# Chunk-selecting attention with a gMLP block: two instead of four head pairs as row halves, half of the stores from GpSimd, and another written-out order

## The chip, the cores and the metric

The kernel runs on one core of a Trainium2 chip. The metric is the device time of one execution in microseconds. A core has five engines that run their own instruction streams and meet only through semaphores: TensorE (PE; matmuls and transposes into PSUM), VectorE (DVE), ScalarE (ACT; exponentials, GELU, evacuation of PSUM), GpSimd (POOL) and SyncE (SP, which here only issues DMAs). The five runs of the kernel before took 216.78 to 218.61 us, median 218.06 us.

## The reference

The input is q, k, v of shape (4, 8, 768, 64): four batches, eight heads, 768 positions. Attention sees only six chunks of 32 keys for each query. They are chosen by an upper bound of the scores:

```python
k_min = np.min(k_chunks, axis=3); k_max = np.max(k_chunks, axis=3)
ub = np.sum(np.maximum(q[:, :, :, None, :] * k_min[:, :, None, :, :],
                       q[:, :, :, None, :] * k_max[:, :, None, :, :]), axis=-1)
ub = np.where(causal, ub, -1e9)
top_chunks = np.argsort(ub, axis=-1)[..., -top_k:]
scores = np.where(sel & (pos[:, None] >= pos[None, :]), scale * q @ k^T, -1e9)
attention = softmax(scores) @ v
```

The heads are then put side by side, x of shape (4, 768, 512), and go through a gMLP block:

```python
h = gelu(x @ w_in)                      # 512 -> 1024, then halves u and v
v_n = (v - mean(v)) / sqrt(var(v) + 1e-6) * g_ln
v_s = einsum('ts,bsd->btd', w_sg, v_n) + b_sg   # 768 x 768 over the positions
out = x + (u * v_s) @ w_out
```

## The kernel before

The 32 heads are taken in 16 pairs; four pairs make one batch, and one gMLP block (b = 0 to 3) follows each four pairs. Every step of the work is one named operation (`P.op`, line 142), a short run of instructions on one engine. A table `ORDER` (from line 18) holds all names in one sequence. `arrange` (L183) walks it, appends each operation to its engine's stream, gives it the PSUM tile number that stands behind the colon, and puts it on another engine where the name carries `@dve`, `@act` or `@pool`. `link` (L214) works out the semaphore waits. So the order on each engine is fixed by the table, and an engine that waits holds back all that stands behind it on that engine. The numbers `cost=` and `prio=` were read by the search that wrote the table; on the chip they do nothing. `FILL` puts a few dummy matmuls (L1041) ahead of some operations, once their PSUM tile is free.

The names, with p a pair, h a head, b a block:

- `lk`, `lq`, `lv` (L499): loads of k, q, v, each head by itself, 192 KB, issued by SP. At most six of them are in flight (`WINDOW`): each waits for the sixth before it to land.
- `kt`, `qt` (L509 to L545): transposes of half a pair's k or q by TensorE. `kn`, `kx` (L530) are the chunk minima and maxima on DVE, `kw` (L541) their difference. `qe`, `qr` (L519, L555 to L564) write q transposed, and its positive part.
- `ub` (L614) makes the upper bounds of one or two pairs in PSUM. `ut`, `uc`, `um`, `ud`, `uq` (L623 to L648, all DVE) transpose them, cut the future, find the sixth largest, and write a row mask `Dt`. Pairs 0 and 1 are selected alone, all others two by two.
- Scores, two ways. `pair_half` (L677, pairs below `NHALF`): k and q of both heads stay as one tile of 128 rows (`KP`, `QP`, written by `ke` and `qc`), and the two heads' products are matmuls over 64 rows each, placed in the upper and lower half of the array (L726). The mask is added by extra matmuls over 32 rows (L719) that read `Dt` directly. One tile `s2.0` holds both heads. `head_full` (L743, all other pairs): head by head, the mask rows sit with k and q in one operand of 96 or 128 rows (`KA`, `QA` or `KB`, `QB`), so one matmul does both (L766). For that `ka`/`kb` evacuate k in two pieces, `qa`/`qb` (L570, L572) copy q, and the rows of `Dt` are copied into `QA` and `QB` by four small DMAs a pair, `d2.00` to `d15.11` (L658, SP), 18 KB each.
- `e` (L736, L770): the exponential on ACT. There are two PSUM tiles of scores, so the second tile after this one waits for it. `af` (L672, POOL): the causal triangle on the diagonal blocks. `vc` (L577, POOL): v to bf16.
- `pv`, `pd` (L787, L795): values, off and on the diagonal. `xr`, `xs` (L804, L813): division by the sum. `xt` (L819): the transpose of x, by SP's transposing DMA, or by TensorE with the copy `xe` for batch 0 and the last one.
- gMLP: `hv` (L853) the v half for 128 positions, four matmuls of 512 columns; `gv` GELU; `bs`, `ba`, `re`, `rp`, `rm`, `rn`, `vh` (L863 to L891) the normalization; `hu`, `gu` (L900, L906) the u half; `pt` (L920) the product with w_sg, six matmuls of 384 columns; `vs`, `gm` (L927, L933) scale, bias and gate; `ou` (L943) the product with w_out, four matmuls; `oa` (L950, DVE) adds x into one of three buffers `osb`; `os` (L955) stores it, 256 KB, from SP. These operations share four PSUM tiles with the transposes, `ub` and `pv`.
- Weights: `win`, `wsg`, `wo` (L962 to L990) are loaded by GpSimd. `wt`, `we` (L980, L985): w_sg transposed by TensorE, six blocks, copied by DVE.

A gMLP operation may stand anywhere in the table among those of the next pairs' attention. In the table before, the first `hv` stands after the selection of pairs 4 to 7 (`ub4`, `ub6`) and after the tiles of heads 8 and 10.

## Time and profile before

| | |
|---|---|
| five runs, median | 218.06 us (216.78 to 218.61) |
| the profiled execution | 216.78 us |
| its span, first to last instruction | 215.0 us |
| PE, DVE, ACT, POOL busy | 202.9, 174.2, 170.5, 118.3 us |
| TensorE's granted clock, mean | 0.995 |
| HBM read and written | 24.77 and 6.29 MB |

The page gives for each engine the time in which it had an instruction running. Matmuls overlap their predecessors' ends, so the record of one is longer than the step from one to the next: a pt matmul is recorded with 326 ns, while 48 of them in a row took 7.80 us, 163 ns each. Costs of TensorE's work are therefore taken from the chain of work that ended last, which lists pieces by the steps between them (start, length, engine, line, how many instructions). In that chain, "SPq" is an issue by SP, and a piece "DMA" is the time from an issue to its landing. A row of a DMA's issue gives the median time to landing.

### The profile page before, as it was taken

How to read it: one execution, taken by the hardware profiler on the slowest of the kernel's cores; microseconds unless marked ns; L12 is line 12 of the kernel's file. 1: busy time of each engine (PE TensorE's matmuls, PEld its weight loads, DVE VectorE, ACT ScalarE, POOL GpSimd, SP SyncE). 2: the span in 40 equal slices, each digit the busy share in tenths (PEclk: the TensorE clock that was granted, in tenths of full speed). 3: DMA queues.
4: the chain of work that ended last, by engine and by line, in shares of the span. 5: the costliest groups of instructions: out<-in, count | busy, mean ns of one | idle time of the engine just before them, and what ended most of it. 6: DMA issues, size and time to landing. Idle time of an engine off the chain costs nothing.

```text
span 215.0 us, 6168 instructions
## 1 busy us (share of the span) xinstructions
PE 202.9 (94%) x2362; PEld 132.1 (61%) x2362; DVE 174.2 (81%) x544; ACT 170.5 (79%) x287; POOL 118.3 (55%) x177
## 2 busy tenths in 40 slices
PE   6688998999999999999999999999999999999990
PEld 2456765567667776865566778764657787445640
DVE  1999999998897978899979999889896558584871
ACT  2469899999989999988998788999997888377000
POOL 3242858968776897915415898303737667030530
PEclk9999999999999999999999999999999999999997
DMA  7999999999889979999469852910172303403034
GB/s 148 220 218 199 213 234 218 147 171 176 155 195 193 216 129 182 268 129 228 94 172 241 204 138 51 232 40 2 38 181 70 109 34 77 146 0 146 5 146 148
DMA packets 92542, 31.78 MB, mean 148 GB/s; under 512 B 85984, under 2 KB 88800, under 8 KB 92512
## 3 DMA queue, kind: packets, MB, share of 16 engines
q1 hardware_dynamic: 90496, 28.62, 61.4%
q0 software_dynamic: 2016, 2.75, 8.7%
q8 instruction: 19, 0.31, 0.6%
q14 instruction: 11, 0.09, 0.1%
HBM read 24.77 MB, written 6.29 MB: 144 GB/s over the span
## 4 chain that ended last, share of the span: by engine, by line
PE 69%; ACT 14%; DVE 7%; DMA 5%; SPq 2%; issue 1%; DVEq 0%
PE PSG L920 14%; PE PSC L766 11%; PE PSG L512 8%; PE PSG L853 7%; PE PSG L943 6%; PE PSG L787 6%; PE PSG L900 5%; PE PSG L614 3%; DMA out_dram<-osb 3%; ACT uT L906 3%; PE PSC L726 3%; PE PSC L719 2%; PE PSG L795 2%; DMA qn<-in_q_dram 2%; ACT E L770 2%; ACT L1046 2%
## 5 line engine op out<-in xcount | busy, mean ns | idle before, releaser
L770 ACT ACTIVATE E<-PSC 128x1024 bf16<-128x1024 f32 (+1 forms) x72 | 62.4, 917 | 7.7 <-PE PSC L766 7.3
L672 POOL TENSOR_SCALAR_AFFINE_SELECT E<-E 128x768 bf16<-128x768 bf16 (+3 forms) x40 | 29.5, 749 | 19.2 <-ACT E L770 10.8
L530 DVE TENSOR_REDUCE W<-PSG 128x12 f32<-128x384 f32 x64 | 34.0, 545 | 4.6 <-PE PSG L512 4.1
L920 PE MATMUL PSG<-wsgT,vhat 128*128 128x384 bf16 x192 | 35.2, 326 | 0.2 <-DVE vhat L891 0.2
L933 POOL TENSOR_TENSOR uT<-vsT,uT 128x384 bf16<-128x384 f32 x24 | 22.6, 950 | 12.7 <-DVE vsT L927 12.4
L927 DVE SCALAR_TENSOR_TENSOR vsT<-PSG,glnT,bsgbc 128x384 f32<-128x384 f32 x32 | 19.6, 611 | 10.5 <-PE PSG L920 10.4
L920 PEld LDWEIGHTS PSG<-wsgT,vhat 128*128 128x128 bf16 x192 | 18.0, 98 | 10.8 <-DVE vhat L891 0.4
L943 PE MATMUL PSG<-woutb,uT 128*128 128x512 bf16 x96 | 23.8, 379 | 0.0
L736 ACT ACTIVATE E<-PSC 128x1024 bf16<-128x1024 f32 (+3 forms) x26 | 21.7, 864 | 2.6 <-PE PSC L726 2.3
L900 PE MATMUL PSG<-xT,winb 128*128 128x384 bf16 x128 | 22.6, 326 | 0.0
L853 PE MATMUL PSG<-winb,xT 128*128 128x512 bf16 x96 | 22.0, 379 | 0.4 <-DVE osb L950 0.4
L577 POOL CAST vx<-vn 128x768 bf16<-128x768 f32 x16 | 13.6, 849 | 14.8 <-DMA vn<-in_v_dram 14.8
L950 DVE TENSOR_TENSOR osb<-PSG,XS 128x512 f32<-128x512 f32 x24 | 16.5, 688 | 5.5 <-PE PSG L943 3.8
L787 PE MATMUL PSG<-vx,E 128*128 128x65 bf16 x480 | 19.7, 193 | 0.6 <-ACT qT L519 0.6
L787 PEld LDWEIGHTS PSG<-vx,E 128*128 128x128 bf16 x480 | 17.7, 97 | 2.9 <-ACT qT L519 0.8
L766 PE MATMUL PSC<-QB,KB 128*128 128x128 bf16 (+2 forms) x168 | 19.1, 246 | 0.3 <-ACT E L770 0.3
L766 PE MATMUL PSC<-QA,KA 96*128 96x128 bf16 (+2 forms) x168 | 19.0, 245 | 0.3 <-ACT E L770 0.3
L858 ACT ACTIVATE vgb<-PSG 128x512 f32<-128x512 f32 x24 | 13.9, 594 | 5.4 <-PE PSG L853 5.3
L873 POOL TENSOR_TENSOR rstd<-rstd,neghalf 128x3 f32<-128x3 f32 x8 | 7.1, 891 | 20.0 <-DVE rstd L869 10.2
L900 PEld LDWEIGHTS PSG<-xT,winb 128*128 128x128 bf16 x128 | 12.4, 98 | 9.2 <-ACT uT L906 0.4
L863 DVE BATCH_NORM_STATS2 stats<-vgb 128x6 f32<-128x512 f32 x24 | 15.8, 678 | 1.8 <-ACT vgb L858 1.6
L512 PE MATMUL PSG<-identF,kn 128*128 128x128 f32 x96 | 15.5, 279 | 1.1 <-DMA kn<-in_k_dram 0.5
(85 smaller groups left out, 389.8 us busy)
## 6 DMA issues: line engine op xcount, KB each, us to landing
kn<-in_k_dram SPq DMA_DIRECT2D x32, 192.0 KB, 4.4
qn<-in_q_dram SPq DMA_DIRECT2D x32, 192.0 KB, 4.4
vn<-in_v_dram SPq DMA_DIRECT2D x32, 192.0 KB, 4.1
out_dram<-osb SPq DMA_DIRECT2D x24, 256.0 KB, 2.7
winb<-in_moe_w_in_dram POOLq DMA_DIRECT2D x4, 256.0 KB, 6.4
vhat<-in_moe_w_sg_dram POOLq DMA_DIRECT2D x3, 192.0 KB, 4.3
xT<-in_moe_w_sg_dram POOLq DMA_DIRECT2D x3, 192.0 KB, 5.9
woutb<-in_moe_w_out_dram POOLq DMA_DIRECT2D x4, 128.0 KB, 4.3
```

The lines of the kernel that those rows point to most:

```text
L512: r = e.matmul(t.ap()[:, 128 * j:128 * j + 128], src[:, 3 * hf + j].rearrange("p i d -> p (i d)"), identF[:], is_transpose=True)
L530: P.op(f"k{'nx'[m]}{p}.{hf}", "dve", lambda d, t=t, m=m, op=op, cs=cs: d.tensor_reduce(W[w][:, m, cs.start // 32:cs.stop // 32], t.ap()[:, ...
L672: P.op(f"af{h}.{r}", "pool", lambda g, ev=ev, cnt=cnt: g.affine_select(ev, ev, pattern=[[0, cnt], [1, 128]], compare_op=ALU.is_ge, fill=0. ...
L736: P.op(f"e{p}.{c}", "act", lambda e, t=t, o0=o0, nn=nn: e.activation(E[:, slot:slot + 2, o0:o0 + nn], t.ap().rearrange("p (i x) -> p i x", ...
L766: r = e.matmul(t.ap()[:, o:o + n], kt_[rows, 128 * kb:128 * kb + 128], qt_[rows, q0:q0 + n], start=True, stop=True, skip_group_check=True)
L770: P.op(f"e{h}h.{c}", "act", lambda e, t=t, c0=c0, c1=c1: e.activation(E[:, es, c0:c1], t.ap()[:, 0:c1 - c0], ACTF.Exp, scale=SCALE), write ...
L787: r = e.matmul(t.ap()[:, 65 * qb:65 * qb + 65], E[:, es, a:a + 128], vx[w][:, kb, i, :], start=first, stop=False, skip_group_check=True)
L853: r = e.matmul(t.ap()[:, 0:F], xT[s][:, dk, 128 * qt:128 * qt + 128], winb[:, dk, F:DFF], start=(dk == 0), stop=(dk == NDK - 1))
L900: r = e.matmul(t.ap()[:, 0:TG], winb[:, dk, 128 * fb:128 * fb + 128], xT[s][:, dk, TG * tg:TG * tg + TG], start=(dk == 0), stop=(dk == NDK ...
L920: r = e.matmul(t.ap()[:, 0:TG], vhat[s][:, sb, 128 * fb:128 * fb + 128], wsgT[:, sb, TG * tg:TG * tg + TG], start=(sb == 0), stop=(sb == N ...
L933: return d.tensor_tensor(gT[s][:, fb, TG * tg:TG * tg + TG], vsT[vs][:], uT[s][:, fb, TG * tg:TG * tg + TG], op=ALU.mult)
L943: r = e.matmul(t.ap()[:, 0:DM], gT[s][:, fb, 128 * qt:128 * qt + 128], woutb[:, fb, :], start=(fb == 0), stop=(fb == NF - 1))
```

## The change

- `NHALF` goes from 4 to 2: pairs 2 and 3 use `head_full`; they get `ka`/`kb`, `qa`/`qb` and the `d` copies. They are selected with 288 query columns instead of 320.
- `WPE` goes from all six to blocks 0, 1, 2: `wt3`, `wt4`, `wt5` become transposing DMAs on SP.
- One load `lv` for both heads of a pair. The buffer `vn` is laid out by head, and `vc` reads it rearranged.
- `hv`, `pt` and `ou` become two operations each (`hv`+`hw`: three and one matmul; `pt`+`pu`: three and three; `ou`+`ov`: two and two) in the same PSUM tile; each piece waits only for its own inputs. Their matmuls are as many as before.
- A store may be issued by GpSimd (`os...@pool`). Eleven are: os0.1, os0.5, os1.3, os1.4, os1.5, os2.1 to os2.4, os3.0, os3.1.
- Two `rT` buffers instead of three, smaller selection buffers, and a dummy matmul that reads 128 columns four times over instead of 512 columns.
- `KDMA = 16` and the buffers `KS` belong to a path for pairs from 16 on, of which there are none.
- The whole table `ORDER`, and `FILL`, are others. The first `hv` now stands ahead of the preparation of pairs 6 and 7 (in part), of `ub6`, and of the tiles of heads 8 and 10. The last gMLP block's `ou` pieces stand between its `pt` pieces.

```diff
-FILL = {"kt1.1": 7, "kt0.1": 4, "qt0.1": 1, "qt2.1": 3, "ou3.4": 1, }
+FILL = {"kt1.1": 7, "kt0.0": 4, "qt0.1": 4, "qt2.0": 3, "s0.2": 1, "ub2": 1, }
...
+                if o.dma is not None:
+                    self.dma_sems[o.dma].remove(o.idx)
+                    o.dma += "_" + eng
+                    self.dma_sems.setdefault(o.dma, []).append(o.idx)
...
-    NHALF = 4
+    NHALF = 2
...
-    WPE = range(NT)
+    WPE = (0, 1, 2)
...
+            if nm == "vn":
+                P.op(f"lv{p}", "sp", lambda e: e.dma_start(
+                    dst[s][:], bass.AP(src.tensor, 2 * p * S * DH, [[DH, 128], [128 * DH, 2 * NT], [1, DH]])),
+                    writes=[(nm, s, 0), (nm, s, 1)], dma=f"{nm}{s}", bulk=True, cost=(640, 1780), prio=prio)
+                return
...
-                def hv(e, t=t, qt=qt):
-                    for dk in range(NDK):
...
+                for nm, dks in (("hv", range(NDK - 1)), ("hw", (NDK - 1,))):
+                    def hv(e, t=t, qt=qt, dks=dks):
+                        for dk in dks:
...
+                    P.op(f"{nm}{b}.{qt}", "pe", hv, reads=[("xT", s, dk, qt // 3) for dk in dks] +
+                         [("winb", dk) for dk in dks], alloc=[t] if nm == "hv" else [], ps=[] if nm == "hv" else [t],
+                         cost=c_pe([F] * len(dks)), prio=prio + qt)
...
+                    for nm, sbs in (("pt", range(3)), ("pu", range(3, NT))):
...
+                    for nm, fbs in (("ou", range(2)), ("ov", range(2, NF))):
...
+                    P.op(f"os{b}.{qt}", "sp", store, reads=[("osb", os_)], dma=f"o{os_}", cost=(640, 500), prio=pq,
+                         alt={"pool": dict(fn=store, cost=(600, 500))})
```

The end of the new table, from the last block's first `pt` on, and of the old one from its last two `pt` on:

```diff
-pt3.11:3 vs3.10 gm3.03 pt3.13:0 gm3.10@dve pt3.12:2 vs3.11 vs3.13 gm3.11 ou3.1:1 vs3.12 ou3.0:3 oa3.1 gm3.12 ou3.2:0
-os3.1 oa3.0 gm3.13 os3.0 oa3.2 ou3.4:2 os3.2 ou3.3:1 oa3.4 ou3.5:3 os3.4 oa3.3 os3.3 oa3.5 os3.5
+rp3.1 pt3.01:2 gu3.20 hu3.10:1 gu3.01 rn3.1 os2.4@pool vh3.4@dve pt3.00:0 gu3.10 pt3.10:3 vh3.3@dve vh3.5 pt3.02:1
+pu3.00 pu3.01 vs3.00 pu3.02 vs3.01 gm3.00 pu3.10 vs3.02 pt3.03:0 gm3.01 pu3.03 pt3.11:2 vs3.03 gm3.02 pu3.11 vs3.10
+ou3.2:1 gm3.03@dve ou3.0:0 pt3.13:3 vs3.11 gm3.10 ov3.0 pu3.13 oa3.0 gm3.11 ou3.1:2 vs3.13 ov3.2 ov3.1 oa3.2 gm3.13
+pt3.12:0 oa3.1 pu3.12 os3.2 os3.0@pool ou3.4:3 vs3.12 ou3.3:1 os3.1@pool ou3.5:2 gm3.12@dve ov3.5 ov3.3 oa3.5 ov3.4
+oa3.3 os3.5 oa3.4 os3.3 os3.4
```

The stretch of the new table between the selection of pairs 2 and 3 and the first tile of head 4:

```
uc2.10 uq2.0 qt4.0:1 af0.1 e0.6 um2.1 kt4.0:0 d2.01 af2.2 s1.0:1 qe4.0 af1.1 kb3.0 kn4.0 d2.00 win2 qt4.1:1 e1.0 ud2.1
d3.00 kt4.1:2 vx10 af1.0 s1.3:0 uq2.1 kx4.0 kb3.1 qb2 d2.11 s1.2:1 e1.3 ka4.0@dve lq5.1 pv1:3 af3.0 kn4.1 d2.10 pd1
e1.2 af0.2 kb4.0@dve s1.6:0 d3.11 iA0 kx4.1 e1.6 pv0:0 d3.01 xr1 s1.4:1 xs1 ka4.1 af3.1 lq5.0 pd0 vc1 e1.4 s4h.1:0 xr0
```

## The prediction

> **What bounds the kernel now.** I read the page first, then the busy time cut at the places where the gMLP blocks begin, then the chain that ended last, and the rows of single shapes last.
>
> ```profile
> span 215.0 us, 6168 instructions
> PE 202.9 (94%) x2362; PEld 132.1 (61%) x2362; DVE 174.2 (81%) x544; ACT 170.5 (79%) x287; POOL 118.3 (55%) x177
> PE 69%; ACT 14%; DVE 7%; DMA 5%; SPq 2%; issue 1%; DVEq 0%
> ```
>
> TensorE has 12.1 us of its span without work, and the chain runs over it for 69%. Where these 12.1 us lie shows in stretches of time (columns: PE, its weight loads, DVE, ACT and POOL busy, granted clock, DMA share, GB/s):
>
> ```profile
> 0.00:15.50 15.50, 11.41 (x112) 6.17 (x112) 10.27 (x45) 7.16 (x15) 5.67 (x16) 1.00 1.15 194
> 15.50:55.08 39.58, 38.03 (x684) 26.09 (x684) 36.83 (x135) 37.34 (x62) 26.77 (x47) 1.00 1.05 194
> 55.08:98.60 43.52, 43.52 (x478) 30.06 (x477) 36.69 (x97) 40.78 (x77) 32.53 (x44) 1.00 0.99 186
> 98.60:184.50 85.90, 85.00 (x961) 57.07 (x960) 72.06 (x232) 75.54 (x117) 46.20 (x62) 1.00 0.50 120
> 184.50:209.90 25.40, 24.98 (x134) 12.76 (x133) 17.62 (x37) 9.64 (x18) 7.11 (x9) 1.00 0.21 76
> 209.90:215.00 5.10, 0.00 (x0) 0.00 (x0) 0.69 (x1) 0.00 (x0) 0.00 (x0) 0.78 0.40 147
> ...
> 62.30:84.00 21.70, 21.70 (x228) 15.79 (x227) 17.48 (x54) 21.43 (x41) 17.67 (x24) 1.00 0.90 182
> ```
>
> Idle TensorE: 4.1 us at the start, 1.6 us up to the first gMLP, 0, 0.9, 0.4, and 5.1 us after the last matmul. So TensorE's work is the time, except in the head and the tail. But the reader should see the last row too: ACT is busy for 21.43 of 21.70 us inside the first gMLP. What leaves TensorE there counts only if ACT has less to do as well.
>
> **The change, part by part.** The sum is made against the profiled execution: 216.8 us, span 215.0 us, 1.8 us around it. The median of the five runs is 218.06 us, 1.3 us above it; I carry the difference over to the median.
>
> *Pairs 2 and 3 as full heads.* Twelve half tiles leave TensorE. In the chain each is a mask piece (L719) and a product piece (L726); three of them:
>
> ```profile
> 38.74 0.32 PE PSC L719 x4
> 39.06 0.33 PE PSC L726 x4
> ...
> 41.24 0.32 PE PSC L726 x4
> ...
> 42.04 0.33 PE PSC L719 x6
> 42.37 0.33 PE PSC L726 x6
> ...
> 50.71 0.60 PE PSC L766 x7
> ...
> 51.50 0.44 PE PSC L766 x4
> ...
> 53.85 0.45 PE PSC L766 x7
> 54.29 0.67 PE PSG L980 x12
> 54.97 0.28 PE PSC L766 x3
> ```
>
> The twelve L719 pieces between 34.5 and 47.7 us add up to 3.36 us, the twelve L726 pieces to 3.63 us: 6.99 us for two pairs. A full head is three tiles of 0.45, 0.44 and 0.28 us, 1.17 us; four heads cost 4.68 us. TensorE gains 2.3 us, and the chain of before passes through all of it.
>
> A rule that speaks against this: the Trainium skill, "TensorEngine Tiling (Array Packing)", Theoretical Speedup, says that a contraction of at most 64 rows, packed in tiles, runs up to twice as fast. By it the 21,504 packed columns of these pairs would take 4.5 us at 2.4 columns per ns, and dropping them would bring nothing. The trace disagrees: 1,024 packed columns took 0.32 us (L726 at 41.24), as many unpacked ones 0.44 us, 1.4 times the pace and not twice. The measurement decides.
>
> *Transposes of w_sg.* Three of six go from TensorE to the transposing DMA: 12 matmuls are 0.67 us above, so six are 0.335 us, three blocks 1.0 us. Their copies (L985, 544 ns) leave DVE. SP issues three transposes more at 1.25 us each (the row of xT<-XS); pt0.10, the first that reads them, stands more than twelve operations of TensorE later in the new order, so a landing of 2.8 us is covered. If it were not, pt would wait up to 2.8 us.
>
> *Selection of pairs 2 and 3* with 288 columns instead of 320: 1.24 to 1.13 us on TensorE, 0.1 us. *The dummy matmul ahead of ou3.4* goes: 216 ns, 0.2 us. Five other dummies are added ahead of 15 us and around ub2, in waits for loads and tile slots; if those waits are gone, they cost 5 x 0.216 = 1.1 us; I take 0.
>
> *hv, pt and ou in two pieces.* No matmul is added; only what a piece waits for is less. In before, ACT and hu tiles filled these waits, so I take 0, but for one place:
>
> ```profile
> 181.17 0.47 SPq L823
> 181.69 4.10 DMA out_dram<-osb
> 185.82 0.70 DVE osb L950
> 186.57 4.49 PE PSG L853 x20
> ```
>
> A store behind a transposing DMA held a buffer, the addition behind it held a PSUM tile, and TensorE waited some 0.5 us before hv3.0. The new order issues that store (os2.1) from GpSimd, and puts ou pieces in front of hv3. I take -0.4 (0 to -0.5).
>
> *Eight Dt copies more.* Full heads read the selection rows from QA and QB, so pairs 2 and 3 now wait for uq, an SP issue and a landing. In the first 60 us such copies landed in 3.8 to 6.1 us, median 4.8, behind the loads, and an issue takes 0.6 us. Head 4 needs two: 2 x 0.6 + 4.8 = 6.0 us. TensorE's work between uq2.0 and s4h.1 in the new order is qt4 and kt4 (4 x 0.33), five tiles of pair 1 (2.6 us) and pv1, pd1, pv0, pd0 (1.3 us): 5.2 us of cover. So I take +0.8; below, 0 (a landing of 2.3 us, the median of QB<-Dt); above, 6.1 + 1.2 - 5.2 = 2.1 us for each of four heads, 8.4 us. Queued on SP behind a late copy are the loads of q for pair 5 and of v for pairs 2 and 3; qt5.1 stands more than ten operations later.
>
> *Where the first gMLP lies.* It begins before pairs 6 and 7 are prepared. Six exponentials (four of 1.02, two of 0.70 us: 5.5 us) and about 1 us of evacuations come into the stretch that has ACT at 94%; TensorE gets 4.4 us more there (two heads 2.3, selection 1.1, seven transposes 2.3, less four such operations that leave, 1.3). ACT goes to 47.3 us beside 47.9 us of TensorE. That can be no wait at all; above, if ACT keeps the 2.7 us of idle time that it has there now, 47.3 + 2.7 - 47.9 = 2.1 us, and 3.0 us with the evacuations that wait for DVE. I take +0.8, below the middle, as 40.78 of 43.52 us made TensorE wait for nothing. The stretch ahead of it has, by the same rows, 7.4 us less ACT and 7.9 us less DVE against 7.5 us less TensorE: no gain, no loss.
>
> *Eleven stores by GpSimd.* An issue is 0.55 us (row of the w_out DMAs), 6.1 us in all; with two qa/qb copies for each qc and three gm more, POOL gets some 10.6 us, beside 97 us of idle time. What is late is the buffer. At the end os3.0 and os3.1 queue on POOL behind gm3.13 (0.91 us) and oa3.3, oa3.4 need their buffers. Counted from pt3.12's start, os3.1 is issued by 1.0 us; oa3.4 could start at 4.1 us. A landing of 2.0 us (SP's stores at the end) is hidden, 4.3 us (the w_out loads on POOL's queue) costs 1.2, 6.4 us (w_in) 3.3 us. The three additions (0.61 us apart) also end 0.3 us further behind TensorE than now. I take +0.5 (0.3 to 3.6), nearest to SP's store, since size and direction are the same.
>
> The Trainium skill, "DMA: Bandwidth & Descriptors", SWDGE vs HWDGE vs iDMA, would leave plain copies to SP, as GpSimd builds descriptors in software; its fit (Anatomy of one DMA) of 2.0 us plus bytes over 436 GB/s gives an estimate of 2.6 us for 256 KB, by which the term would be +0.3. No row here shows a store by GpSimd.
>
> *Merged v loads, casts reading v by head, no early ones on half pairs:* SP issues 16 fewer; POOL waited 14.8 us for v without anyone on the chain waiting for POOL. 0 (-0.3 to +0.5).
>
> Sum: -2.3 - 1.0 - 0.1 - 0.2 - 0.4 + 0.8 + 0.8 + 0.5 = -1.9 us: span 213.1, profiled run 214.9, median 216.1 us.
>
> **Rivals.**
> - *ACT takes over* from 15 to 95 us. ACT's work there falls by 0.8 us only, TensorE's by 3.1. For it: 21.43 of 21.70 us busy. Against: over 15.5 to 98.6 us ACT still idles 5 us. The 2.3 us between them are lost in place of the 0.8 above: 217.6 us, no change; with the 3.0 us of its upper end 218.3.
> - *Slower: the Dt rows of pairs 2 and 3 come late*, between 28 and 40 us. For it: 4.8 us landing with the DMA queues at 1.05 share. Against: by 24 us the first 24 loads are through (192 KB at 217 GB/s, 0.9 us each), and a wait for head 4 gives cover to head 5. With 1.4 us for each of four heads, 5.6 in place of 0.8: 220.9 us. From 1.0 us a head (3.9 us in all) it is slower by over 0.5%.
> - *GpSimd's stores land like w_in*, 6.4 us: 3.6 in place of 0.5: 219.2 us; at 4.3 us 217.1.
> - *Everything is covered*: no wait for Dt, none for ACT: 214.4 us.
>
> **How the numbers follow.** Forecast 0.47 (own range 214.9 to 217.4), ACT 0.19, Dt rows 0.14, stores 0.07, all covered 0.13. About 0.5%, 1.1 us, is what a measurement of this kernel can tell; its five runs lie 1.8 us apart. Below 217.0: of the forecast 0.39, all covered 0.13, of ACT and stores 0.04: 0.56. Above 219.1: Dt rows 0.13, the slow ends of ACT and of the stores 0.10: 0.23. Between: 0.21. The range goes from a little under the covered case (0.07 left out) to the middle of the slow cases (0.12 left out): 213.4 to 219.9 us.
>
> **What would show it.** After: TensorE's idle time around 12 us with 3.4 us less work; no L719 after 30 us; L766 ahead of 30 us without an idle time put down to QA<-Dt; the first L853 near 47 us; ACT's busy share from there above 95%, TensorE's idle time there below 1.5 us; the GpSimd stores' landing near 3 us, and the last additions without a wait for out_dram. It is wrong if TensorE idles over 3 us between 15 and 47 us (Dt rows), over 2 us in the first gMLP (ACT), or if DVE waits for out_dram by more than 2 us in all.

## The result and the profile after

The changed kernel took 218.7 us (median of 38 executions, 214.9 to 221.8), the kernel before 217.39 us (median of 75, on the same chips). The ratio is 0.998 with a 95% interval of 0.9956 to 1.0001: no change that this measurement can tell, where 216.1 us and a gain of 0.9% were forecast. (Medians here and below are over all executions; ratios and their intervals leave out those over 1.5% above the fastest of their kernel, here 27 of the changed kernel's 38, and by the medians it is 0.6% slower.) The profiled execution of the changed kernel took 220.9 us; it is longer than the median by 2.2 us, and a second profile of the same kernel below (219.3 us, span 217.5) shows the same picture in the same places.

What TensorE waited or lost is counted in the text from the steps between the starts of its matmuls. That gives some 0.2 us more for each wait than the tables of waits do, because the record of a matmul outlasts its step.

The page of the changed kernel: its span, the engines' busy time, the rows of 40 slices for TensorE, its granted clock and the DMA engines, and the chain's shares.

```profile
span 219.2 us, 6002 instructions
...
PE 204.4 (93%) x2288; PEld 137.5 (63%) x2288; DVE 171.0 (78%) x539; ACT 170.3 (78%) x283; POOL 128.4 (59%) x193
...
PE   6898689999998999997999999999999999999990
...
PEclk9999955799999999999999999999999999999999
DMA  7999966999187899996789439997101152421033
...
PE 78%; DMA 7%; DVE 7%; SPq 2%; ACT 2%; issue 1%; DVEq 0%
```

TensorE has less to do and is busy for longer, 204.4 us against 202.9. The clock row says why: slices 6 to 8 are not at 9. Stretches of time of the same kernel (columns as in the prediction: length, PE, its weight loads, DVE, ACT, POOL busy, granted clock, DMA share, GB/s), cut where the clock changes and where the gMLP blocks begin:

```profile
15.50:27.35 11.85, 9.02 (x157) 5.63 (x157) 11.20 (x56) 10.72 (x18) 9.70 (x19) 1.00 1.11 204
27.35:41.00 13.65, 12.79 (x143) 9.64 (x144) 7.64 (x22) 7.84 (x12) 6.34 (x13) 0.50 0.76 154
41.00:53.20 12.20, 12.02 (x235) 10.12 (x233) 10.04 (x25) 11.89 (x21) 11.33 (x17) 1.00 1.14 219
53.20:103.90 50.70, 48.48 (x544) 33.82 (x541) 43.45 (x130) 47.03 (x82) 32.63 (x46) 1.00 0.87 164
103.90:150.70 46.80, 46.48 (x534) 32.33 (x526) 41.68 (x128) 43.56 (x73) 25.34 (x35) 1.00 0.84 177
150.70:190.00 39.30, 39.30 (x453) 26.20 (x446) 29.26 (x103) 33.72 (x48) 26.34 (x36) 1.00 0.31 84
190.00:213.80 23.80, 23.76 (x133) 12.34 (x129) 16.68 (x38) 8.25 (x16) 10.03 (x14) 1.00 0.18 67
213.80:219.20 5.40, 0.00 (x0) 0.00 (x0) 1.03 (x2) 0.00 (x0) 0.00 (x0) 0.93 0.39 147
```

For 13.65 us, ahead of the first gMLP block, TensorE ran at half of its clock; before, it had the full clock from the start to the last matmul. The first `hv` stands at 53.2 us, where about 47 was expected, and the first gMLP stretch takes 50.7 us, where the prediction's working gives 48.7 (47.9 of TensorE and 0.8 of waits). From 104 us on the kernel goes as forecast or a little better. What TensorE waited for most between 15.5 and 53 us, from the table of its waits (engine, line, what ended the wait; us in all, times, longest):

```profile
PE PSG L531 <- DMA kn<-in_k_dram: 1.8, 1, 1.8
PE PSC L747 <- DVE Dt L676: 1.3, 2, 1.0
```

And the chain in front of the longer one (start, length, what):

```profile
17.80 0.55 SPq L516
18.34 0.04 issue
18.39 1.54 SPq L522
19.93 0.04 issue
19.97 1.04 SPq L516
21.01 0.04 issue
21.05 7.02 DMA kn<-in_k_dram
28.07 0.14 issue
28.21 0.87 PE PSG L531 x3
```

L531 is a transpose, here `kt4.0`; its k (`lk4.1`) was issued at 21.05 us, behind both merged v loads (L516) and a q load, and landed 7.0 us later. The other wait is `s1.1`'s, for the row mask of pair 1 (L676), which DVE makes in a stretch where it is busy for 11.20 of 11.85 us.

Some steps of the prediction can be read directly. The half tiles (L747 and L754 here) end with pair 1. No wait of TensorE here is for `QA<-Dt`. The issue rows of the stores:

```profile
out_dram<-osb SPq DMA_DIRECT2D x13, 256.0 KB, 2.3
out_dram<-osb POOLq DMA_DIRECT2D x11, 256.0 KB, 2.8
```

GpSimd's stores land in 2.8 us, SP's in 2.3, and the tail after the last matmul is 5.4 us against 5.1.

### The profile page after: what moved, and what is told of

It is laid out like the page before. It is cut to its first block, busy times and chain, and to the rows that moved or that the text cites. A ratio compares the mean times of both kernels' runs of the same rounds, so it can differ in the third digit from the quotient of the medians.

```text
span 219.2 us, 6002 instructions
## 1 busy us (share of the span) xinstructions
PE 204.4 (93%) x2288; PEld 137.5 (63%) x2288; DVE 171.0 (78%) x539; ACT 170.3 (78%) x283; POOL 128.4 (59%) x193
## 4 chain that ended last, share of the span: by engine, by line
PE 78%; DMA 7%; DVE 7%; SPq 2%; ACT 2%; issue 1%; DVEq 0%
PE PSG L950 14%; PE PSC L794 14%; PE PSG L881 9%; PE PSG L929 9%; PE PSG L531 8%; PE PSG L975 7%; PE PSG L815 6%; DMA kn<-in_k_dram 5%; PE PSG L642 3%; DMA out_dram<-osb 3%; PE PSG L823 2%; DVE osb L982 2%; SPq L522 1%; PE PSC L754 1%; DVE W L549 1%
## 5 line engine op out<-in xcount | busy, mean ns | idle before, releaser
L798 ACT ACTIVATE E<-PSC 128x1024 bf16<-128x1024 f32 (+1 forms) x84 | 73.7, 919 | 6.5 <-PE PSC L794 5.8
L950 PE MATMUL PSG<-wsgT,vhat 128*128 128x384 bf16 x192 | 38.0, 326 | 0.4 <-DVE KB L540 0.3
L964 POOL TENSOR_TENSOR uT<-vsT,uT 128x384 bf16<-128x384 f32 x27 | 25.0, 934 | 9.1 <-DVE vsT L958 9.0
L975 PE MATMUL PSG<-woutb,uT 128*128 128x512 bf16 x96 | 25.8, 379 | 0.0
L794 PE MATMUL PSC<-QA,KA 96*128 96x128 bf16 (+2 forms) x196 | 24.1, 254 | 0.0
L794 PE MATMUL PSC<-QB,KB 128*128 128x128 bf16 (+2 forms) x196 | 22.7, 246 | 0.0
L531 PE MATMUL PSG<-identF,kn 128*128 128x128 f32 x96 | 17.3, 299 | 2.3 <-DMA kn<-in_k_dram 2.3
L794 PEld LDWEIGHTS PSC<-QA,KA 96*128 96x128 bf16 x196 | 15.3, 101 | 5.6 <-issue 0.6
L794 PEld LDWEIGHTS PSC<-QB,KB 128*128 128x128 bf16 x196 | 14.6, 98 | 5.4 <-issue 0.5
L599 POOL CAST QB<-qT 64x768 bf16<-64x768 f32 x14 | 11.7, 838 | 10.0 <-ACT qT L538 9.4
```

What stands on the lines that cost most here:

```text
L531: r = e.matmul(t.ap()[:, 128 * j:128 * j + 128], src[:, 3 * hf + j].rearrange("p i d -> p (i d)"), identF[:], is_transpose=True)
L794: r = e.matmul(t.ap()[:, o:o + n], kt_[rows, 128 * kb:128 * kb + 128], qt_[rows, q0:q0 + n], start=True, stop=True, skip_group_check=True)
L798: P.op(f"e{h}h.{c}", "act", lambda e, t=t, c0=c0, c1=c1: e.activation(E[:, es, c0:c1], t.ap()[:, 0:c1 - c0], ACTF.Exp, scale=SCALE), write ...
L950: r = e.matmul(t.ap()[:, 0:TG], vhat[s][:, sb, 128 * fb:128 * fb + 128], wsgT[:, sb, TG * tg:TG * tg + TG], start=(sb == 0), stop=(sb == N ...
L964: return d.tensor_tensor(gT[s][:, fb, TG * tg:TG * tg + TG], vsT[vs][:], uT[s][:, fb, TG * tg:TG * tg + TG], op=ALU.mult)
L975: r = e.matmul(t.ap()[:, 0:DM], gT[s][:, fb, 128 * qt:128 * qt + 128], woutb[:, fb, :], start=(fb == 0), stop=(fb == NF - 1), skip_group_c ...
```

## The experiments

Two theories went first. *Clock*: the two early waits cost little themselves, but they make the chip halve TensorE's clock. *ACT*: the gain is lost in the first gMLP, which ACT fills. All ratios are to the kernel before, run beside it on the same chip.

**The changed kernel again (e0_after).** No edit; 12 executions.

> The changed kernel once more, on the chip of the runs beside it. Theory gate: TensorE's granted clock is 0.5 for some 10 to 14 us between 24 and 41 us in most executions, its time stays within 0.5% of before (ratio 0.995 to 1.005). Theory ACT (the first gMLP block, where ACT is full, takes the gain): the same ratio, and executions without a half clock are no shorter than those with one.

Measured: 218.42 us (216.14 to 221.9), ratio 1.0009 [0.9974, 1.0044]. Profile: span 217.5 us, clock 0.5 from 26.1 us for 13.65 us again. Over its 12 executions the mean clock lay between 0.961 and 0.992; 35 executions of the kernel before had 0.991 to 1.0. Most executions lose their clock, not only the profiled ones.

**Dummy matmuls in the two waits (e1_fill).**

```diff
-FILL = {"kt1.1": 7, "kt0.0": 4, "qt0.1": 4, "qt2.0": 3, "s0.2": 1, "ub2": 1, }
+FILL = {"kt1.1": 7, "kt0.0": 4, "qt0.1": 4, "qt2.0": 3, "s0.2": 1, "ub2": 1, "s1.1": 4, "kt4.0": 9, }
```

> Dummy matmuls are put into the two waits of TensorE ahead of the half clock: 4 ahead of s1.1, 9 ahead of kt4.0. Nothing else changes, and TensorE still waits as long for the k load of pair 4. Theory gate: no half clock between 10 us and the end, the first hv starts near 48 us instead of 53, the span is some 4 us shorter than the changed kernel's (ratio to before 0.975 to 0.985). Theory ACT: under 1 us shorter, ratio 0.993 to 1.0, since ACT sets the pace from 16 us on.

Measured: 217.3 us (215.58 to 219.68), ratio 0.9973 [0.9938, 1.0008], span 214.4 us. The clock row of its page:

```profile
PEclk9999999999999999999999999999999999999999
```

More work on TensorE, and 1.1 us less in the median than e0_after, 3.1 us less in the profile. (The intervals of the two ratios overlap, so the 1.1 us are rough.) The first gMLP stretch is 49.5 us here as in e0_after, so what was gained lies ahead of it. (The 50.7 us of the first profile hold a wait of 1.4 us near the stretch's end, at `pv14`, for an addition that waited for a store's buffer; one later profile, e12_q6_only, has it again.) But the median is only level with the kernel before: the clock is one part.

**An earlier k for pair 4 (e2_loads).** On SP: lk4.0 **lk4.1** lq4.1 **lq4.0** lv0 lk5.0 lv1 lk5.1.

```diff
-... lk4.0 ... lk5.0 ... lq4.1 ... lv0 ... lq4.0 ... lv1 ... lk4.1 ... lk5.1
+... lk4.0 ... lk4.1 ... lq4.1 ... lq4.0 ... lv0 ... lk5.0 ... lv1 ... lk5.1
```

> Five loads change places: the second k load of pair 4 and the first q load go ahead of the two double v loads. Theory gate: the 2.0 us wait ahead of kt4.0 goes, and with it the half clock: 4 to 6 us shorter than the changed kernel, ratio to before 0.970 to 0.985. If the clock halves all the same (the 1.0 us wait ahead of s1.1 stays), only the 2 us wait is won. Theory ACT: under 1 us shorter.

Measured: 217.99 us (214.93 to 220.17), ratio 0.9975 [0.9934, 1.0016]. `kt4.0` no longer waits, yet the clock is halved from 26.4 us for 10.24 us. TensorE's waits of 0.5 us and more between 15.5 and 50 us:

```profile
PE PSC L747 <- DVE Dt L676: 1.0, 1, 1.0
PE PSG L531 <- ACT KA L538: 0.7, 1, 0.7
PE PSG L642 <- POOL W L568: 0.6, 1, 0.6
```

And the clock row of the page:

```profile
PEclk9999956999999999999999999999999999999998
```

Waits of 1.0 us and less, the longest of them 2 us ahead of the fall, were enough here.

**All stores from SP (e3_sp_stores).** The eleven `@pool` behind `os` names taken away.

> All 24 stores go from SP again, at the same places in the order. If the stores by GpSimd took the gain (additions waiting for a buffer), this is 1 to 3 us shorter than the changed kernel. Theories gate and ACT: within 0.7 us of it, and the half clock is there as before.

Measured: 217.92 us (215.77 to 221.68), ratio 0.9996 [0.9961, 1.0031]; span 214.6 us with 6.83 us of half clock from 27.9 us; tail 5.2 us. Who issues the stores makes no difference that shows.

**Three w_sg transposes on SP, alone, in the kernel before (e4_before_wt).**

```diff
-    WPE = range(NT)
+    WPE = (0, 1, 2)
```

(with `we3`, `we4`, `we5` taken out of the table).

> The kernel before, with one part of the change alone: three of its six w_sg transposes (wt3, wt4, wt5) go from TensorE to SP's transposing DMA. My prediction's term: TensorE's path loses 12 matmuls, 1.0 us, so the median falls from 217.3 by 0.6 to 1.1 us (ratio 0.995 to 0.997), and the span of an undisturbed profile from 215.0 to about 214.0. Rival (SP's queue has no room): the three issues of 1.25 us hold loads behind them on SP between 45 and 85 us, TensorE waits for pair 8 and later, and nothing is gained (ratio 0.999 or more), with a wait for a load (in_k_dram, in_q_dram or wsg) ending a TensorE idle time of over 0.5 us between 60 and 100 us.

Measured: 222.12 us (217.67 to 224.33). The ratio, 1.0071 [1.0015, 1.0127], rests on two of twelve executions; by the medians it is 1.023. The rival's direction, and more than its size: the part takes 1.0 us from TensorE's work, and it cost 4.9 us. But the mechanism is not the rival's: TensorE did not wait for a load that an issue held up, but for a transposing DMA itself. The landings of the three transposing DMAs, from the view of the tile `wsgT`:

```profile
DMA to landing us min/median/max: 3.2/5.8/6.5
```

`wt4` was issued at 74.4 us, `pt0.10` needed it and could start at 80.3, 3.7 us late, and then the clock was halved, as the stretch of time behind it shows:

```profile
81.66:85.07 3.41, 3.41 (x38) 3.22 (x36) 1.62 (x4) 3.02 (x9) 1.73 (x2) 0.50 0.04 7
```

In the order before nothing covers this landing of 5.8 us; the prediction had reckoned with 2.8.

**Both early waits dealt with (e5_loads_fill).** e2's order of loads, and in `FILL` `"s1.1": 4`.

> The changed kernel with both of the early TensorE waits dealt with: the loads of k for pair 4 ahead of the merged v loads on SP (as in e2_loads, where the 1.97 us wait of kt4.0 went), and four dummy matmuls ahead of s1.1, in the wait of 1.0 us for pair 1's Dt rows (as in e1_fill). Gate theory (a TensorE that idles for some 2 us inside about 4 us near 25 us loses its full clock for 3.4 to 13.7 us): no half clock between 15 and 200 us in the profile, mean clock 0.98 or more, the first gMLP begins near 49 us and the span is 213 to 214.5; median 216.0 to 217.0, ratio 0.990 to 0.996. If the half clock comes from elsewhere (as in e2_loads, where one wait of 1.0 us was left), it is there again near 26 us, the span is 216 or more, and the ratio 0.997 to 1.001. ACT theory (the first gMLP stretch is what ate the gain): the stretch between hv0 and hv1 stays 49.5 us or more in either case, and the median stays within 0.3% of before.

Measured: 217.4 us (214.48 to 219.0, 12 executions), ratio 0.995 [0.9915, 0.9984]; span 212.7 us, clock 0.995, no half clock until the last matmul. The profile is what the prediction worked out (213.1 us), the median is not. The first gMLP stretch is 49.3 us.

**Two more profiles of the same kernel (e5b_look, e5c_look).**

> e5_loads_fill once more, for a profile: its twelve executions lay between 214.5 and 219.0 us with a clock of 0.98 or more, and the profile was of the fastest. If this one is 216.5 us or more with a clock of 0.99 or more, the time over the first look must be in waits of TensorE that the first did not have. Theory of the loads: these waits are ended by in_k_dram, in_q_dram, in_v_dram or Dt copies behind them on SP, between 15 and 70 us, and the stretches after 97 us are the same within 0.5 us. Rival (half clock in short windows): the excess is at a clock of 0.5.

> A third look at e5_loads_fill, as e5b_look: the theory of the loads says that the place of the excess over the first look changes from execution to execution (another load or Dt copy each time), but stays between 15 and 70 us; a fixed place and size in both looks would speak for one wait that only the first look did not have.

Measured: 216.5 and 213.67 us, spans 214.8 and 211.9, clock 0.993 and 1.0. Of the 2.8 us between them 0.8 lie ahead of 15 us, and the rest is in one place. TensorE stood still ahead of `qt6.1` for 0.6, 0.8 and 2.6 us in executions of 213.7, 214.5 and 216.5 us, and in all three the wait ended with the landing of `lq6.0`, at 42.1, 42.9 and 45.3 us. The wait in e5b_look (the profile names no releaser; the landing is read from the DMA's own record):

```profile
PE PSG L531 <- issue: 2.5, 1, 2.5
```

A fixed place and a load: the loads have no slack there.

**v loads in two again (e6_split_v).** Each `lv` as two loads of 192 KB.

```diff
-                P.op(f"lv{p}", "sp", lambda e: e.dma_start(
-                    dst[s][:], bass.AP(src.tensor, 2 * p * S * DH, [[DH, 128], [128 * DH, 2 * NT], [1, DH]])),
+                for i in range(2):
+                    P.op(f"lv{p}.{i}", "sp", lambda e, i=i: e.dma_start(
+                        dst[s][:, i], bass.AP(src.tensor, (2 * p + i) * S * DH, [[DH, 128], [128 * DH, NT], [1, DH]])),
```

> The changed kernel with each v load as two loads of one head each again (16 issues more on SP), all else as it is. Theory (the merged load of 384 KB is what stands ahead of lk4.1 in the queues): the bytes ahead of lk4.1 are the same, so kt4.0 still waits 1 to 2 us and the half clock near 26 us stays: 218 to 219 us, ratio 1.000 to 1.004. Rival (one large DMA holds the DMA engines longer than two small ones, or its issue of 1.0 to 1.5 us on SP is what is late): lk4.1 lands earlier by 0.5 us or more, the wait of kt4.0 falls under 1 us, and the ratio goes to 0.997 or less. Against that, 16 issues more on SP could hold later loads: then a wait for in_k_dram or in_q_dram after 50 us grows.

Measured: 217.98 us (216.31 to 221.51), ratio 1.0003 [0.9976, 1.0031]. Nine of twelve executions had a mean clock of 0.961 to 0.978. The profiled one (0.993) is one of the others: it has the waits of `s1.1` and `kt4.0`, as long and as far apart as in e0_after (1.0 and 1.0 us there), and no half clock before the last matmul:

```profile
PE PSC L748 <- DVE Dt L677: 1.0, 1, 1.0
PE PSG L532 <- DMA kn<-in_k_dram: 0.9, 1, 0.9
```

Merging the loads as such is worth nothing either way; their place is what counts.

**A late k in the kernel before (e7_before_late_k).** The places of `lk4.0` and `lq4.1` exchanged.

> The kernel before, with the places of two loads exchanged in SP's order (lk4.0, the first k of pair 4, and lq4.1), so that kt4.1 gets its k some 2 to 3 us later. Gate theory: TensorE gets a wait of 1 to 2.5 us near 30 us, and if the wait comes with another one within 4 us, the granted clock is 0.5 for 3.4 to 13.7 us in this kernel too; mean clock 0.96 to 0.99, span 217 to 220, median 219 to 221 (ratio 1.006 to 1.018). If only the wait itself costs (the clock stays at 1.0, because a single wait under 2 us does not trip it): ratio 1.004 to 1.010, span about 216.5. If nothing waits (the load had slack), the ratio is 1.000, and the run says nothing of the clock.

Measured: 221.66 us (219.74 to 222.35), ratio 1.0166 [1.0126, 1.0207]. TensorE's longest wait between 15 and 30 us:

```profile
PE PSG L512 <- DVE W L530: 1.9, 1, 1.9
```

It is the wait of `kt4.1`, and it ended when `lk4.0` landed, at 22.43 us by the DMA's own record, 0.1 us ahead of the start; the reduction that the table names had ended before.

And the stretch of time right behind it:

```profile
22.66:29.49 6.83, 6.83 (x94) 4.76 (x93) 3.32 (x9) 3.94 (x7) 3.25 (x9) 0.50 0.86 179
```

One wait of 1.9 us, 1.5 more than in the same place before (0.4), and the span grew by 4.9 us: the clock theory holds in the other kernel too, and it is not a matter of the changed order.

**The five added dummies taken away (e8_no_fill).**

```diff
-FILL = {"kt1.1": 7, "kt0.0": 4, "qt0.1": 4, "qt2.0": 3, "s0.2": 1, "ub2": 1, }
+FILL = {"kt1.1": 7, "kt0.0": 4, "qt0.1": 1, "qt2.0": 3, }
```

> The changed kernel without the five dummy matmuls that the change adds (qt0.1 has 1 in place of 4, s0.2 and ub2 none). My prediction took their cost as 0, in waits that are there anyway, and at most 1.1 us. If that was right, TensorE reaches the end of ub2 at the same time within 0.2 us, and the median is that of the changed kernel within 0.3 us (218.0 to 218.7). If they cost their time, it is faster by 0.5 to 1.1 us (217.3 to 217.9). Gate theory: with longer idle times of TensorE between 14 and 23 us, and the waits of s1.1 and kt4.0 as before, the half clock comes as early or earlier and lasts as long or longer: 218.5 to 220, mean clock 0.96 to 0.975 in most executions.

Measured: 218.46 us (216.75 to 220.7), ratio 1.0038 [1.0009, 1.0067]. `s0.1` starts at 22.18 us with this edit and at 22.32 us without it, in e0_after: the dummies cost 0.1 us, where 0 was taken. Half clock of 10.24 us from 26.6 us in the profile.

**The three w_sg transposes back on TensorE (e10_wt_pe)**, in e5_loads_fill, at free tiles among the first `pt`.

```diff
-    WPE = (0, 1, 2)
+    WPE = range(NT)
```

> e5_loads_fill with the three w_sg transposes taken back to TensorE (three more blocks of six matmuls, three more copies on DVE, three transposing DMAs less on SP), inside the first gMLP. My prediction's term: TensorE's path gains 3 x 0.335 us, so the first gMLP stretch grows from 49.3 to 50.3 us and the time by 1.0 us against e5_loads_fill (span of an undisturbed profile 213.7, median 218.4, ratio 0.999 to 1.000). Rival (what the issues on SP delay costs as much as they save, as in e4_before_wt): no more than 0.3 us slower than e5_loads_fill in the median (217.1 to 217.7), with a narrower spread, as no transposing DMA stands between the loads of pairs 8 to 10.

Measured: 220.48 us (219.76 to 221.72), ratio 1.0159 [1.0126, 1.0193]. Its first gMLP stretch, which is where the transposes stand, against the same stretch of e17_two_first at the end of this list (49.30 us, as in e5_loads_fill):

```profile
51.40:103.20 51.80, 49.63 (x554) 34.54 (x557) 45.40 (x133) 47.29 (x82) 31.31 (x45) 1.00 0.78 151
```

2.5 us longer: TensorE is busy for 1.9 us more, 1.0 of it the three blocks, and idle for 0.6 more; the rest I put down to the tiles at the places that I gave them. So in the changed order the term is, by this one profile each, no worse than the prediction had it, and its rival falls. The rest of the difference to e5_loads_fill lies ahead of 51 us, where both kernels have the same instructions: 3.2 us of waiting for `qt6.1`, and 3.41 us of half clock behind it. It is the late load again.

**q of pair 6 ahead of a v load (e11_q6_early)**, in e5_loads_fill.

```diff
-... lq6.1 ... lv3 ... lq6.0 ... lk6.1
+... lq6.1 ... lq6.0 ... lv3 ... lk6.1
```

In the kernel `lv3` is the v of pair 3 and `lv2` that of pair 2; the expectations here and of e14_loads_first and e17_two_first name other pairs.

> e5_loads_fill with one more pair of loads exchanged on SP: the second q load of pair 6 (lq6.0) ahead of the merged v load of pairs 6 and 7 (lv3). In three looks at e5_loads_fill TensorE's wait for qt6.1 was 0.6, 0.8 and 2.6 us and ended when lq6.0 landed (42.1, 42.9, 45.3 us), and these three executions took 213.7, 214.5 and 216.5 us. Theory of the loads (the rest of the gain is lost to loads that land when they are needed): lq6.0 lands some 1 to 3 us earlier, the wait goes to under 0.3 us in the profile, and the median falls to 214.5 to 216 (ratio 0.987 to 0.994) with a narrower spread. Rival (the queues as a whole are the bound up to 48 us, so that what one load gains the next one loses): the wait moves to pv6, pv7 (v of pairs 6 and 7) or kt6.1 with the same size, and the ratio stays at 0.995 to 0.998.

Measured: 216.04 us (214.8 to 217.31), ratio 0.9955 [0.9928, 0.9982]; all twelve clocks 0.993 or more. `qt6.1` waits 0.28 us. But in the profile the wait has moved to v:

```profile
PE PSG L815 <- POOL vx L604: 1.2, 1, 1.2
PE PSG L823 <- POOL E L700: 1.2, 1, 1.2
```

Both theories have a part of this: faster and steadier, with 3.2 us still lost between 40 and 50 us.

**The same exchange alone, in the changed kernel (e12_q6_only).**

> The changed kernel with only this exchange (lq6.0 ahead of lv3), the two early waits left in. Both theories: the half clock near 27 us stays, and as it holds TensorE's work back by 3 to 5 us ahead of 42 us, the load of q for pair 6 has slack there anyhow: 217.5 to 218.7 us, ratio 0.999 to 1.003. If it gains as much as e11_q6_early gains on e5_loads_fill, the half clock was not what mattered.

Measured: 218.38 us (216.45 to 220.12), ratio 1.0039 [1.001, 1.0067]; eight of twelve clocks between 0.955 and 0.970. The exchange brings nothing here, as expected, while in e11_q6_early it came with a gain: where the clock falls, this load has slack. The profiled execution kept its clock (0.996); in it `lk4.1` landed at 25.65 us, early enough, and `kt4.0` did not wait.

**One copy of DVE earlier in the first gMLP (e13_q6_kb)**, in e11_q6_early: `kb7.0` ahead of `kx7.1`.

> e11_q6_early with one place in the first gMLP changed: DVE's copy kb7.0, which frees a PSUM tile for ub6, goes ahead of kx7.1 on DVE (and so is done some 0.5 us earlier). In all looks at the changed kernel TensorE lost 0.61 us at pt0.00 and 0.42 us at ub6, at this place. If it is the tile: TensorE loses under 0.6 us there in place of 1.0, and the stretch of the first gMLP falls from 49.3 to 48.8 us; the median 0.3 to 0.5 us under that of e11_q6_early. If ACT sets the pace of the stretch (my prediction's rival), it stays at 49.3 us.

Measured: 216.49 us (215.7 to 220.36), ratio 0.9968 [0.9947, 0.999]; the stretch 49.5 us, the loss at this place 1.2 us, not less. Its only wait in the table over the stretch:

```profile
PE PSG L642 <- POOL W L568: 1.1, 1, 1.1
```

In e17_two_first, with the order as it was, the same wait of `ub6` ends with the tile, `kb7.0`:

```profile
PE PSG L642 <- DVE KB L540: 0.4, 1, 0.4
```

With the exchange `kx7.1` ends later on DVE, and `kw7` (L568), the width of pair 7's k chunks, can only follow it. So `ub6` needs both operations of DVE and waits for whichever stands second; ACT ends neither wait. (The second place, behind `ub6`, is `pt0.01`, not `pt0.00` as the expectation has it.)

**Three loads ahead of the rows of Dt (e14_loads_first)**, in e11_q6_early. In the kernel before no Dt copy stands on SP between 15 and 38 us; it issued its loads with two waits of under 1 us, and the last k or q load of pairs 0 to 7 landed at 40.2 us. In the changed kernel it landed at 52.0. SP's longest waits between 15 and 50 us there:

```profile
SPq L686 <- DVE Dt L676: 3.5, 1, 3.5
SPq L522 <- PE PSG L531: 2.6, 1, 2.6
```

SP stands 3.5 us for a row of pair 2, with the loads of pairs 5 to 7 behind it.

```diff
-... lk5.1 ... d2.01 ... d2.00 ... d3.00 ... d2.11 ... lq5.1 ... d2.10 ... d3.11 ... d3.01 ... lq5.0 ... lv2 ... d3.10
+... lk5.1 lq5.1 lq5.0 lv2 ... d2.01 ... d2.00 ... d3.00 ... d2.11 ... d2.10 ... d3.11 ... d3.01 ... d3.10
```

> e11_q6_early with three loads on SP taken ahead of the eight Dt copies of pairs 2 and 3 (both q loads of pair 5 and the merged v load of pairs 4 and 5), so that they are issued near 25 us instead of 29 to 33 us. In the kernel before, no Dt copy stands on SP between 15 and 38 us, and all loads of pairs 0 to 7 have landed by 39.7 us; in the changed kernel SP waits up to 3.5 us for the first of these rows, and the same loads land up to 50 us. Theory of SP's order (the Dt copies hold the loads, and the loads hold TensorE near 42 us): the loads of pairs 6 and 7 land 2 to 4 us earlier (lk6.0 by 44 instead of 46.2 us), TensorE's loss between 40 and 50 us falls from 3.2 to under 1.5 us, and the median from 216.0 to 214 to 215.3 us (ratio 0.985 to 0.991). Rival (the term that my prediction had for the Dt rows): the copies now stand behind 768 KB of loads in the queue and land 1.5 to 3.5 us later, and s4h to s7h wait for them, 1 to 4 us in all, so that nothing is gained or it is slower (ratio 0.995 to 1.010).

Measured: 216.34 us (214.56 to 219.23, 7 executions), ratio 0.9936 [0.9905, 0.9966]; span 212.8 us. Both came true. `lk6.0` landed at 44.5 us instead of 46.2, and TensorE's loss between 40 and 50 us fell from 3.2 to 0.8 us. But the first row landed 6.1 us after its issue instead of 4.1, and TensorE waited for it:

```profile
PE PSC L794 <- DMA QA<-Dt: 1.3, 1, 1.3
```

Six of the seven executions had a mean clock of 0.979 to 0.988, under the 0.991 to 1.0 of the kernel before; the profiled one, the fastest, had 0.995. So in most of them the clock fell somewhere, and part of this median is the clock's.

**The rows from GpSimd (e16_dt_pool)**, in e11_q6_early: the eight `d2` and `d3` copies issued by GpSimd at the same places.

```diff
-... d2.01 af2.2 ... d2.00 win2 ... d3.00 ... d2.11 ...
+... d2.01@pool af2.2 ... d2.00@pool win2 ... d3.00@pool ... d2.11@pool ...
```

> e11_q6_early with the eight Dt copies of pairs 2 and 3 issued by GpSimd instead of SP, at the same places of the order. Theory of SP's order: SP issues the loads of pairs 5 to 7 without a stop from 22 us on, they land 3 us or more earlier, TensorE's loss between 40 and 50 us falls from 3.2 to under 1.5 us; if GpSimd's masks and copies behind the waiting Dt issue are not what TensorE needs, the median falls to 214 to 215.3 us (ratio 0.985 to 0.991). Rival: GpSimd stops for 2 to 4 us on the first row, its masks (af1, af2, af3) and v casts come late and pv0 to pv3 wait for them, or the Dt rows land later from its queue: ratio 0.996 or more.

Measured: 218.59 us (217.15 to 219.41), ratio 1.004 [1.0013, 1.0066]. The loads are early (`lk6.0` lands at 40.1 us), and the rival's waits are there, for the masks and the v casts that stand behind the rows on GpSimd. GpSimd itself stood only 0.7 us for the first row; its eight issues of 0.5 us each stand among the masks and casts. Then the clock falls to 0.5 for 6.83 us from 35.1 us on. TensorE's two largest waits up to 100 us (the lines are one further down in this kernel):

```profile
PE PSG L824 <- POOL E L701: 1.6, 2, 1.0
PE PSG L816 <- POOL vx L604: 1.5, 1, 1.5
```

**The rows between the loads (e17_two_first)**, in e11_q6_early.

```diff
-... lk5.1 ... d2.01 ... d2.00 ... d3.00 ... d2.11 ... lq5.1 ... d2.10 ... d3.11 ... d3.01 ... lq5.0 ... lv2 ... d3.10
+... lk5.1 lq5.1 lq5.0 ... d2.01 ... d2.00 ... d3.00 ... d2.11 ... lv2 ... d2.10 ... d3.11 ... d3.01 ... d3.10
```

> Between e11_q6_early and e14_loads_first: only the two q loads of pair 5 go ahead of the Dt copies on SP, and the merged v load of pairs 4 and 5 stands between them, behind the three rows that heads 4 and 5 need first and d3.00. In e14_loads_first the first row (d2.01) landed at 33.6 us, right behind that v load (33.4), and TensorE waited 1.5 us for it ahead of s4h.1; in e11_q6_early it landed at 30.7 us, but TensorE lost 3.2 us between 40 and 50 us to late loads. Theory (rows and loads share one queue, and only their order is the fault): the row lands near 32 us, s4h.1 waits under 0.4 us, TensorE's loss between 30 and 50 us falls from 3.1 (e14_loads_first) or 4.4 (e11_q6_early) to under 2.5 us, and the median falls to 214.3 to 215.8 us, ratio 0.985 to 0.992. Rival (the queue is full whatever the order): the wait comes back at pv4 (v of pair 4) or qt6.1, with 1 to 2 us, and the ratio stays at 0.993 to 0.997.

Measured: 214.35 us (213.37 to 217.25, 6 executions), ratio 0.9854 [0.981, 0.9897], the fastest of all; five of the six executions had a mean clock of 0.993 or more. The page's span and clock rows:

```profile
span 212.6 us, 5995 instructions
...
PEclk9999999999999999999999999999999999999998
```

And its stretches of time up to the second gMLP block:

```profile
15.50:48.00 32.50, 29.50 (x527) 21.80 (x525) 28.94 (x99) 30.23 (x50) 27.16 (x47) 1.00 1.06 205
48.00:97.30 49.30, 47.78 (x536) 33.78 (x539) 43.35 (x129) 46.87 (x82) 32.70 (x46) 1.00 0.93 180
```

The row landed at 32.7 us and `s4h.1` still waited 0.9 us for it, more than the 0.4 expected; the loads landed within 1.0 us of those in e14_loads_first, and TensorE lost 2.8 us between 30 and 50 us, not the 2.5 expected, in place of 3.1 and 4.4. The median came out at the lower edge of what was expected.

## Why the prediction was wrong

**What held.** Where the clock stays and the loads come, the profile is near the sum's: 211.9 and 212.7 us (e5; 214.8 in the one with the late load), 212.6 (e17), against 213.1 worked out. In part that is luck: by the medians e17_two_first gains 3.4 us, where the sum has 1.9, and its order of loads is not the one that was predicted. The twelve tiles of pairs 2 and 3 took 4.68 us in e17_two_first, to the hundredth of the working; the term of -2.3 stands. The w_sg term of -1.0 stands in this order (e10_wt_pe: +2.5 without it, part of it from the places that the transposes were given), although e4_before_wt shows that it was the order's merit: the same edit in the order before cost 4.9 us. The dummies cost 0.1 us, taken as 0. The store term of +0.5 measured 0.3 by the tails, and the hand-over to the last gMLP gained about 0.9 where -0.4 was taken (TensorE's loss between 180 and 200 us went from 0.9 us to nothing).

**ACT in the first gMLP**: +0.8 was taken, 1.5 came. TensorE's 47.9 us were right (47.78 in e17_two_first), ACT's 47.3 were nearly so (46.87), and 1.5 us of idle time were left in 49.3 (2.2 in the changed kernel's own profile, with the 1.4 at `pv14`). But it was the wrong engine: about 1.0 us of the 1.5 stands at `ub6` and `pt0.01`, and there TensorE waits for DVE, as e13_q6_kb shows. The rival "ACT takes over" had 2.3 us lost to ACT; the waits that ACT ended make 0.4 us in e17_two_first.

**The step that failed** is the one on the Dt copies, in the sentence on what is queued behind them: "Queued on SP behind a late copy are the loads of q for pair 5 and of v for pairs 2 and 3; qt5.1 stands more than ten operations later." This priced the loads behind the rows at nothing. I looked for the cost where TensorE waits for a row: that was 0 in the changed kernel, against +0.8 taken. The cost was one queue further: SP stood up to 3.5 us for the first row. The q loads of pair 5 landed 4 and 10 us later than before and the k and q loads of pairs 6 and 7 9 to 16 us later (the last at 52.0 instead of 40.2 us), without slack for pairs 6 and 7. The rows alone hold these loads back by 4 to 6 us: with the rows on GpSimd `lk6.0` landed at 40.1 instead of 46.2 us and `lk7.0` at 46.0 instead of 50.5 (e16_dt_pool against e11_q6_early). The rest I put down to their place in the new table. The same step's neighbour, "Merged v loads ... 0", looked at their number and not at what now stands behind them: `lk4.1`, 7.0 us from issue to landing, and `kt4.0`'s wait.

**And no term was there for the clock.** The prediction read 1.00 in every stretch and let each wait cost its own length. Its sign of being wrong, over 3 us of idle TensorE between 15 and 47 us, did appear (4.0 us), but it was put down to the Dt rows alone. About 3 us of it lay in two waits, for pair 1's mask and for `lk4.1`, of which each looked harmless; in four profiles with these two waits (the changed kernel, e0_after, e3_sp_stores, e8_no_fill) the clock was halved for 6.8 to 13.7 us. What this made of the time is read from the repairs, each against the kernel before beside it, by the medians: dummies in the waits took the changed kernel from +1.1 us (218.42 against 217.34) to level (217.3 against 217.34); with the k load put right in place of most of these dummies it stood at +0.2 us, and the q load, then the rows and loads interleaved, took it to -1.2 and to -3.4 us. So of the 4.4 us between the changed kernel and what its own parts can do, some 1.1 us came with the clock held and some 3.3 with the order of loads and rows on SP. This split goes by the order of the repairs, and the two are not independent: with the clock still falling the q load brought nothing (e12_q6_only), and a late load or row can cost the clock in its turn (e10_wt_pe; by the mean clocks also e14_loads_first). A single ratio is known to some 0.3 to 0.4%, up to 1 us, so the steps are rough; the whole is clear of that.

The early estimate of the first `hv` at 47 us was the same error in another form: "no gain, no loss" in the stretch ahead of it added up the engines' work and asked nothing of the loads. It stands at 53.2 us in the changed kernel and at 48.0 in e17_two_first.

## What to carry to other kernels

When a change puts an instruction that waits onto a queue that issues in order, list what stands behind it and compare each item's issue and landing with the moment of its use, before and after; here the waiting row cost nothing, and the loads behind it, with the clock that fell in two waits, took the gain. A wait of one or two microseconds on TensorE is not always priced by its length: read the granted clock behind it, and if it falls, fill the wait or move what it waits for. One profile of a kernel without slack can be a lucky one; repeated profiles of the same kernel show by the place of the excess which transfer is late.

## What the runs showed of the hardware

- TensorE's granted clock went to 0.5 after quite short idle times: one of 1.9 us (e7_before_late_k), one of 1.0 us with two of 0.6 to 0.7 us ahead of it (e2_loads), and 1.0 and 2.0 us with 2.0 us of work between them (the changed kernel, where it fell 1.1 us into the second). In the 3.41 us ahead of the fall the profile has TensorE idle for 1.0 us in e2_loads, 1.2 in e0_after, 1.3 in the changed kernel and 2.0 in e7_before_late_k. The clock stayed down for 3.41, 6.83, 10.24 or 13.65 us, one to four times 3.41 us.
- The falls stand on a fixed grid. In all nine profiles with a half clock ahead of the last matmul, its start and its end lie a whole number of steps of 3.413 us ahead of the fall that follows the last matmul (56 and 52 steps in the changed kernel, 40 and 39 in e4_before_wt, by the trace's clock records). So the clock changes at fixed moments that do not follow the waits: in two profiles of the changed kernel it fell 1.1 and 0.3 us into the same wait. How a wait lies to these moments may decide whether it costs the clock; no run here separates that.
- The same waits did not always do it. e6_split_v has waits of 1.0 and 0.9 us where e0_after has 1.0 and 1.0, as far apart, and kept its clock in the profile, while nine of its twelve executions did not; in e5b_look a wait of 2.6 us cost none, and in e10_wt_pe one of 3.2 us in the same place did.
- The Trainium skill, "TensorE: Matmul & The Clock Gate", Part 1 (The HAM clock gate), has the clock halved after a window of some 3.4 us in which TensorE idles, with windows that run freely; the lengths and the grid here agree with that. But no wait here that tripped it was as long as the window but the 3.7 us of e4_before_wt. By the same page's advice against gaps of over 3 us (Why this matters for your kernels) only that one and the 3.2 us of e10_wt_pe should have mattered; the runs say that 1.9 us can.
- The half clock did not halve TensorE's pace: its work from `kt4.0` to the end of the first `xt0.0` took 13.04 us in the changed kernel, nearly all of it at half clock, and 8.42 us in e12_q6_only at the full clock, 4.6 us or a factor of 1.55.
- A row of 18 KB landed in 4.1 us behind the usual loads and in 6.1 us behind three more (e11_q6_early, e14_loads_first), 0.2 us after the last of the three: here a small transfer landed in its turn behind the large ones that SP had issued before it.
